# Attention transposes as 64-row halves, the last query tile's scores in 64-row form, and one written order for attention

## The chip, the cores and the metric

The kernel runs on one core of a Trainium2 chip. The metric is the device time of one execution in microseconds (us); the median of three runs of the kernel before is 1041.93 us (1041.54 to 1042.49).

## What is computed

Causal attention with a forget bias over 4 x 8 heads of 576 rows and 64 columns, then two feed-forward layers over the 2304 tokens.

```
B, H, S, D = q.shape                      # 4, 8, 576, 64
scores = scale * np.matmul(q, k.transpose(0, 1, 3, 2))
cum = np.cumsum(np.maximum(s, 0.0), axis=-1)
bias = -(cum[:, :, :, None] - cum[:, :, None, :])
scores = np.where(causal, -1000000000.0, scores + np.minimum(bias, 0.0))
attn = np.exp(scores - np.max(scores, axis=-1, keepdims=True))
attn = attn / (np.sum(attn, axis=-1, keepdims=True) + 1e-09)
attn_out = np.matmul(attn, v)
...
x = np.ascontiguousarray(attn_out.transpose(0, 2, 1, 3)).reshape(B * S, H * D)
x = (1.0 / (1.0 + np.exp(-(x @ w_gate))) * (x @ w_val)) @ w_out
h = x @ w_in
return (h * np.cos(h)) @ w_out2
```

## The kernel before

The program has two stages. `attention` handles 16 pairs of heads, two heads side by side on the 128 partitions. `moe` then runs both feed-forward layers; the change does not touch it.

For one pair p, the 576 query rows are cut into tiles t = 0 to 3 of 128 rows and t = 4 of 64 rows for each head, the two tails of the pair together. The operations have names, which the change's table uses:

- G loads q, k and v; PQ and PK transpose q (five 128 x 128 transposes, L554) and k (six of 96 rows, L551) on TensorE; H and L split the result into a high and a low part (QH, QL, KH, KL, 64 rows to a head). DB spreads the cumulated s over the partitions (CB).
- Z, ZA and ZM make bias and causal mask on GpSimd. A computes scores: A0 is t = 0 and 1, A2 and A3 are t = 2 and 3 (L629: 64 rows of each head, the two heads as two matmuls side by side). A4 is the last tile (L634: one matmul over all 128 rows, with q of the two heads in a block form).
- X adds the bias and takes the row's extreme on VectorE (L646); E is the exponential on ScalarE (L650), which also sums the row; T transposes the result (L688 and L690: 25 transposes to a pair, each one matmul of 128 identity columns over 128 rows). C copies a transposed tile from PSUM to `pt`, on ScalarE (L460) or VectorE (L464).
- V0 and V1 multiply with v (L725, L727: 128 rows, 64 output partitions to a head). U copies that out; RA, RC, RT, RR, RD, RB make the reciprocal of the sums, turn it (L740), write it to memory and read it back spread over the partitions; M divides; XH and XL split the result for `moe`.
- Early pieces of the first weights (w0, w1, w2) are decoded along with it, and 40 "fill" matmuls of 256 columns (L788) stand wherever the planner finds TensorE free; 2 "warm" groups and one group at L475 stand at the start.

What sets the order: `Plan.run` is a list scheduler. It takes, of all operations that could begin within 0.1 us of the earliest, the one of lowest priority number (PRIO, EARLY, the pair's number), and picks ScalarE, VectorE or GpSimd for it by planned end plus a toll. Every engine then executes its own operations in that order, waiting on semaphores. PSUM is eight banks, given out by `Banks` under limits by kind (LIMIT); a T takes one bank of its own, except that of t = 4, which takes two.

Of the kernel before, what the change touches and what calls it, by code (L numbers as in the profile page):

```python
# [24 lines left out]
INF = float("inf")  # L25
# [11 lines left out]
class Buf:  # L37


    def __init__(self, pool, n=1, kind=None):  # L40
        self.pool, self.n, self.kind, self.left, self.slots, self.end = pool, n, kind, 0, None, 0.0
        pool.order.append(self)
# [6 lines left out]
class Pool:  # L49
    def __init__(self, n, fifo=True):  # L50
        self.n, self.fifo = n, fifo
        self.free = [0.0] * n
        self.order, self.next = [], 0

    def when(self, buf):
        if self.fifo and self.order[self.next] is not buf:
            return INF, None
        ok = sorted((t, i) for i, t in enumerate(self.free) if t < INF)
        if len(ok) < buf.n:
            return INF, None  # L60
        return ok[buf.n - 1][0], [i for _, i in ok[:buf.n]]

    def take(self, buf):
        _, slots = self.when(buf)
        buf.slots = sorted(slots)
        for i in slots:
            self.free[i] = INF
        self.next += 1
# [6 lines left out]
class Banks(Pool):  # L75


    def __init__(self, n, limit):
        super().__init__(n, fifo=False)
        self.limit, self.held, self.kinds = limit, {}, {}  # L80

    def when(self, buf):
        free, held = self.free, self.held.setdefault(buf.kind, [])
        lim = self.limit[buf.kind]
        now = sum(1 for t in held if t == INF)
        if now >= lim:
            return INF, None
        at = sorted((t for t in held), reverse=True)[lim - 1] if len(held) >= lim else 0.0
        best = (INF, 0, [])
        for i in range(0, self.n, 2):  # L90
            a, b = free[i], free[i + 1]
            if buf.n == 2:
                best = min(best, (max(a, b, at), 0, [i, i + 1]))
            else:
                for x, y, z in ((a, b, i), (b, a, i + 1)):
                    best = min(best, (max(x, at), -y if y < INF else -1e9, [z]))
        return best[0], best[2]

    def take(self, buf):
        super().take(buf)  # L100
        held = self.held[buf.kind]
        buf.place = len(held)
        held.append(INF)

    def give(self, buf):
        super().give(buf)
        self.held[buf.kind][buf.place] = buf.end


class Op:  # L110
    __slots__ = ("name", "alts", "fn", "prio", "deps", "left", "ready", "begins", "bufs", "out", "unit", "start", "end", "n", "xfer")
# [3 lines left out]
LAT = {"pe": 0.24, "act": 0.16, "dve": 0.13, "pool": 0.08}  # L115


class Plan:
# [3 lines left out]
    def op(self, name, alts, fn, rd=(), wr=(), needs=(), prio=0.0, xfer=0.0):  # L122
        o = Op()
        o.name, o.alts, o.fn, o.prio, o.xfer = name, alts, fn, prio, xfer
        o.n, o.unit, o.start, o.end, o.ready = len(self.ops), None, None, None, 0.0
        deps = set()
# [12 lines left out]
        o.deps, o.left, o.out = deps, len(deps), []  # L139
        for d in deps:  # L140
            d.out.append(o)
        o.bufs = {k[0] if isinstance(k, tuple) else k for k in (*rd, *wr, *needs)}
        o.bufs = [b for b in o.bufs if isinstance(b, Buf)]
        o.begins = []
        for b in o.bufs:
            b.left += 1
            o.begins.append(b)
# [3 lines left out]
    def run(self, slack=0.1):  # L151
        free = {}
        dma = 0.0
        ready = [o for o in self.ops if o.left == 0]
        done = []
        while ready:
            best = None
            cand = []
            for o in ready:
                at = o.ready  # L160
                for b in o.begins:
                    if b.slots is None:
                        t, _ = b.pool.when(b)
                        at = max(at, t)
                if at == INF:
                    continue
                for u, dur in o.alts.items():
                    s = max(at, free.get(u, 0.0))
                    cand.append((s, o, u, dur))
            if not cand:  # L170
                raise RuntimeError("stuck: " + ", ".join(o.name for o in ready[:20]))

            by_op = {}
            for s, o, u, dur in cand:
                c = (s + dur + TOLL.get(u, 0.0), s, o, u, dur)
                if o.n not in by_op or c[0] < by_op[o.n][0]:
                    by_op[o.n] = c
            first = min(c[1] for c in by_op.values())
            _, s, o, u, dur = min((c for c in by_op.values() if c[1] <= first + slack), key=lambda c: (c[2].prio, c[1], c[2].n))
            for b in o.begins:  # L180
                if b.slots is None:
                    b.pool.take(b)
            o.unit, o.start = u, s
            free[u] = s + dur
            if o.xfer:
                dma = max(dma, s + dur) + o.xfer
                o.end = dma + 2.3
            else:
                o.end = s + dur
# [5 lines left out]
            ready.remove(o)  # L195
            done.append(o)
            for d in o.out:
                d.left -= 1
                same = not o.xfer and set(d.alts) == {u}
                d.ready = max(d.ready, o.end + (SAME.get(u, 0.05) if same else LAT.get(u, 0.1)))  # L200
                if d.left == 0:
                    ready.append(d)
        if len(done) < len(self.ops):
            raise RuntimeError("operations left")
        self.done = sorted(done, key=lambda o: (o.start, o.n))
        return self.done


TOLL = {"act": 0.7, "dve": 0.52, "pool": 0.05}
REPORT = None  # L210
W0PRIO = 4

PV_GROUPS = [(0, 1), (2, 3, 4)]

ORDER = [0, 2, 4, 3]
LIMIT = {"prep": 3, "s4": 6, "s": 3, "t4": 2, "t": 4, "v": 4, "r": 6}

PRIO = {
# [4 lines left out]
}  # L223

EARLY = [
    {
# [4 lines left out]
    },  # L231
    {
# [4 lines left out]
    },  # L237
]
WARM = 2
W0AT = 2  # L240
FILL = 40
# [3 lines left out]
def kernel(  # L245
# [168 lines left out]
    def attention():  # L414
        with ExitStack() as c2:
# [6 lines left out]
            OPS = {n: [att.tile([P, S + TAIL if n[0] == "Q" else S], F32R, name=f"{n}{i}") for i in range(NCC)] for n in ("QH", "QL", "KH", "KL")}  # L422
            CB = [[att.tile([P, 6 * P], F32, name=f"CB{e}{i}") for i in range(NCC)] for e in range(2)]
            VN = [att.tile([P, NQ, 2, D], F32, name=f"VN{i}") for i in range(NV)]
            QKN = {x: [att.tile([P, NQ, 2, D] if x == "Q" else [PP, 6, 2, D], F32, name=f"{x}n{i}") for i in range(NQK)] for x in "QK"}
# [18 lines left out]
            pl["pw"] = Banks(8, LIMIT)  # L444
            DMA = {"sp": 0.62}

            here = [2]

            def add(name, alts, fn, prio, rd=(), wr=(), needs=(), xfer=0.0):
# [3 lines left out]
                kind = re.match('[A-Za-z]*', name)[0]  # L453
                o = plan.op(name, alts, None, rd, wr, needs, prio + PRIO.get(kind, 0.0) + (EARLY[here[0]].get(kind, 0.0) if here[0] < 2 else 0.0), xfer)
# [11 lines left out]
            def half(e):  # L466
                return slice(64 * e, 64 * e + 64)

# [23 lines left out]
            def setup_tail(u):  # L492
                for i in range(NQK):
                    for e in range(2):
                        u.memset(QKN["Q"][i][half(1 - e), NT4, e], 0.0)
                for i in range(NV):
                    u.memset(VN[i][TAIL:P, NT4], 0.0)
                for i in range(NPT):
# [562 lines left out]
```

## Time and profile before

| | |
|---|---|
| median of the runs | 1041.93 us |
| the profiled execution | 1041.43 us, of which its span is 1039.6 us |
| attention: first matmul to first matmul of `moe` | 1.18 to 185.03 us |
| `moe` | 185.03 us to the end |
| busy over the span | TensorE 99%, VectorE 70%, ScalarE 45%, GpSimd 40% |
| granted TensorE clock, mean | 1.000 |

The ends of matmuls are modelled, so that a busy TensorE is not one at its peak: what a matmul costs is read from the start of one to the start of the next. A row of the timeline merges instructions of a line that follow each other, so the start of the next row minus its own start, divided by its count, is the cost of one.

### The profile page before, as it was taken

How to read it: one execution, taken by the hardware profiler on the slowest of the kernel's cores; microseconds unless marked ns; L12 is line 12 of the kernel's file. 1: busy time of each engine (PE TensorE's matmuls, PEld its weight loads, DVE VectorE, ACT ScalarE, POOL GpSimd, SP SyncE). 2: the span in 40 equal slices, each digit the busy share in tenths (PEclk: the TensorE clock that was granted, in tenths of full speed). 3: DMA queues.
4: the chain of work that ended last, by engine and by line, in shares of the span. 5: the costliest groups of instructions: out<-in, count | busy, mean ns of one | idle time of the engine just before them, and what ended most of it. 6: DMA issues, size and time to landing. Idle time of an engine off the chain costs nothing.

```text
span 1039.6 us, 16693 instructions
## 1 busy us (share of the span) xinstructions
PE 1029.1 (99%) x6116; PEld 945.9 (91%) x6116; DVE 730.8 (70%) x1406; ACT 472.2 (45%) x1060; POOL 413.2 (40%) x494
## 2 busy tenths in 40 slices
PE   9999999999999999999999999999999999999998
PEld 6776777999999999999999999999999999999997
DVE  7788898565645557744344887888688878886565
ACT  4878877342222222221121335666555455554443
POOL 3567776241222223321111234555255535552222
PEclk9999999999999999999999999999999999999999
DMA  7777784321111111111010111121021101100111
GB/s 170 174 194 166 185 188 103 93 81 41 42 41 41 61 41 61 62 46 37 21 41 21 42 61 61 41 61 61 1 61 41 61 21 42 61 1 13 49 61 61
DMA packets 94802, 70.49 MB, mean 68 GB/s; under 512 B 61888, under 2 KB 82752, under 8 KB 94720
## 3 DMA queue, kind: packets, MB, share of 16 engines
q1 hardware_dynamic: 93456, 69.06, 24.0%
q8 instruction: 48, 0.79, 0.3%
q10 hardware_dynamic: 1264, 0.37, 0.2%
q14 instruction: 34, 0.28, 0.1%
HBM read 64.54 MB, written 4.87 MB: 67 GB/s over the span
## 4 chain that ended last, share of the span: by engine, by line
PE 93%; DVE 2%; issue 2%; DMA 1%; POOL 1%; ACT 1%; SPq 0%; POOLq 0%; DVEq 0%; ACTq 0%
PE pw L381 21%; PE pw L380 21%; PE pw L382 20%; PE pw L908 6%; PE pw L909 6%; PE pw L910 6%; PE pw L727 3%; PE pw L688 3%; PE pw L629 3%; PE pw L634 1%; DMA rb<-rec_d 1%; PE pw L554 1%; PE pw L551 1%; DMA raw<-in_moe_w_gate_dram 0%; DVE pu L646 0%
## 5 line engine op out<-in xcount | busy, mean ns | idle before, releaser
L382 PE MATMUL pw<-XH,wp 128*128 128x384 f32 x960 | 322.7, 336 | 0.0
L381 PE MATMUL pw<-XL,wp 128*128 128x384 f32 x960 | 322.7, 336 | 0.0
L380 PE MATMUL pw<-XH,wp 128*128 128x384 f32 x960 | 322.5, 336 | 0.0
L335 POOL TENSOR_TENSOR wp<-wm,wp 128x512 fp32r<-128x512 f32 x68 | 101.5, 1493 | 228.7 <-DVE wp L334 226.0
L380 PEld LDWEIGHTS pw<-XH,wp 128*128 128x128 f32 x960 | 180.1, 188 | 3.7
L381 PEld LDWEIGHTS pw<-XL,wp 128*128 128x128 f32 x960 | 180.0, 188 | 3.6
L382 PEld LDWEIGHTS pw<-XH,wp 128*128 128x128 f32 x960 | 180.1, 188 | 0.0
L898 POOL TENSOR_TENSOR gl<-tm,gh 128x384 fp32r<-128x384 f32 x96 | 108.8, 1133 | 142.7 <-ACT gh L897 142.6
L327 POOL TENSOR_TENSOR wm<-wm,wx 128x512 int32<-128x512 int32 x68 | 90.4, 1329 | 181.6 <-DVE wm L326 181.6
L826 DVE TENSOR_TENSOR tm<-pw,tm 128x384 f32<-128x384 f32 x72 | 40.1, 557 | 148.8 <-PE pw L382 139.1
L908 PE MATMUL pw<-wp,gh 128*128 128x512 f32 x288 | 112.2, 389 | 0.0
L909 PE MATMUL pw<-wp,gh 128*128 128x512 f32 x288 | 112.1, 389 | 0.0
L910 PE MATMUL pw<-wp,gl 128*128 128x512 f32 x288 | 112.0, 389 | 0.0
L828 ACT CAST gh<-tm 128x384 fp32r<-128x384 f32 x72 | 37.0, 514 | 143.9 <-DVE tm L826 143.9
L883 DVE SCALAR_TENSOR_TENSOR tm<-tm 128x384 f32<-128x384 int32 x96 | 99.0, 1031 | 3.3
L884 ACT ACTIVATE tm<-tm 128x384 f32<-128x384 f32 x96 | 50.6, 527 | 108.9 <-DVE tm L883 108.9
L380 PE MATMUL pw<-gh,wp 128*128 128x384 f32 x288 | 96.7, 336 | 0.6 <-ACT acc L854 0.6
L381 PE MATMUL pw<-gl,wp 128*128 128x384 f32 x288 | 97.0, 337 | 0.0
L382 PE MATMUL pw<-gh,wp 128*128 128x384 f32 x288 | 96.2, 334 | 0.0
L314 ACT ACTIVATE wx<-wx,ebias 128x512 int32<-128x512 int32 x68 | 49.2, 723 | 99.9 <-DVE wx L313 98.8
L650 ACT ACTIVATE pu<-pu,nm 128x128 f32<-128x128 f32 (+3 forms) x144 | 82.8, 577 | 19.8 <-DVE nm L646 19.5
L891 DVE SCALAR_TENSOR_TENSOR tm<-tm,pw 128x384 f32<-128x384 f32 x96 | 52.8, 550 | 42.4 <-ACT tm L885 42.4
(102 smaller groups left out, 1721.0 us busy)
## 6 DMA issues: line engine op xcount, KB each, us to landing
raw<-in_moe_w_out_dram SPq DMA_DIRECT2D x28, 512.0 KB
CB<-cum_d SPq DMA_DIRECT2D x32, 288.0 KB
raw<-in_moe_w_in_dram SPq DMA_DIRECT2D x16, 512.0 KB
raw<-in_moe_w_gate_dram SPq DMA_DIRECT2D x12, 512.0 KB
raw<-in_moe_w_val_dram SPq DMA_DIRECT2D x12, 512.0 KB
VN<-in_v_dram SPq DMA_DIRECT2D x31, 160.0 KB
Kn<-in_k_dram SPq DMA_DIRECT2D x32, 144.0 KB
rb<-rec_d SPq DMA_DIRECT2D x32, 144.0 KB
```

What stands on the lines that cost most here:

```text
L327: pool.tensor_tensor(m, m, st["x"], ALU.add)
L335: pool.tensor_tensor(w[:, 1], m, f(w[:, 0]), ALU.subtract)
L380: pe.matmul(ps, wh, xh, start=first, stop=False)
L381: pe.matmul(ps, wh, xl, start=False, stop=False)
L382: pe.matmul(ps, wl, xh, start=False, stop=last)
L650: act.activation(o, o, AF.Exp, bias=NMT[nm.slot][:, col:col + 1], scale=-1.0, accum_out=SUMS[sums.slot][:, col:col + 1])
L883: dve.scalar_tensor_tensor(r, kk, -TWO_PI_LO, r, ALU.mult, ALU.add)
L891: dve.scalar_tensor_tensor(g, r, -0.5, h, ALU.add, ALU.mult)
L898: pool.tensor_tensor(gl, g, f(gh), ALU.subtract)
L908: pe.matmul(ps, gh[:, ts], w[:, 0], start=it["first"], stop=False)
L909: pe.matmul(ps, gh[:, ts], w[:, 1], start=False, stop=False)
L910: pe.matmul(ps, gl[:, ts], w[:, 0], start=False, stop=it["last"])
```

## The change

Four things change in `attention`, none in `moe`.

1. A transpose (`flip`) becomes two matmuls, one for rows 0 to 63 and one for rows 64 to 127, each with 64 identity columns and the same 128 stationary columns, into two neighbouring PSUM banks. It holds for T, RT and for q and k; k is loaded as 128 x 4 rows and a tail, and so has five transposes in place of six. Before, 400 T, 80 PQ, 96 PK and 16 RT are issued; after, 832 halves for T and RT and 320 for q and k.
2. The last tile's scores (A4) are twelve matmuls of 64 rows, six side by side, in place of six of 128 rows; they come in two halves, A4 and A5, and A5 stands behind T of t = 0 and 1 of the same pair, so that t = 4 is the last of the pair's tiles.
3. The scheduler, its priorities, the limits by kind and the 40 fillers go. A table SEQ names all operations of attention in one order, with the engine where there is a choice (`:a` ScalarE, `:d` VectorE, `:p` GpSimd). T of one group, both heads, shares one pair of PSUM banks.
4. Copies C read the two halves in one instruction; t = 1 takes two copies (one to a head) in place of one, t = 4 one of 640 columns in place of two. K's high and low parts are 640 columns wide in place of 576. K's load is three DMAs to a pair in place of two.

```
+            def flip(out, i, x):
+                for h in range(2):
+                    pe.transpose(out[:, h, i:i + 64], x[half(h)], ident[half(h), half(h)])
...
-                                u.dma_start(out=t, in_=src.rearrange("(c p) d -> p c d", p=PP))
...
+                            u.dma_start(out=t[:, 0:NT4, e], in_=src[e, 0:NT4 * P].rearrange("(p c) d -> p c d", c=NT4))
...
+                        if x == "K":
+                            u.dma_start(out=t[half(0), NT4], in_=src[:, NT4 * P:S].rearrange("e p d -> p e d"))
...
-                    def scores4(u, sc=sc, cc=cc):
-                        for z in range(2):
-                            for i, (a, b) in enumerate(SCP):
-                                pe.matmul(PW[:, sc[0].slot + z, 0:HS], OPS[a][cc.slot][:, NT4 * P:NT4 * P + P], OPS[b][cc.slot][:, z * HS:(z + 1) * HS], start=i == 0, stop=i == 2)
...
+                    def scores4(u, turn, sc=sc, cc=cc):
+                        for i, (a, b) in enumerate(SCP):
+                            for e in range(2):
+                                z = e ^ turn
+                                pe.matmul(PW[:, sc[0].slot + z, 0:HS], OPS[a][cc.slot][half(e), QCOL[NT4]:QCOL[NT4] + P], OPS[b][cc.slot][half(e), z * HS:(z + 1) * HS], start=i == 0 and turn == 0, stop=i == 2 and turn == 1)
...
+                        add(f"A5.{p}", "pe:400", parts[1], rd=[*ready, ("t01", p, 0), ("t01", p, 1)], wr=[sc4])
...
-                                        pe.transpose(o[:, c * P:(c + 1) * P], x[:, c * P:(c + 1) * P], ident)
...
+                                    for c in range(t + 1):
+                                        i = (TAIL + c * P) % S if t == NT4 else c * P
+                                        flip(o, e * (t + 1) * 64 + c * 64, x[:, i:i + P])
...
-            for i in range(FILL):
-                fill = Buf(pl["pw"], 1, "t")
...
-            done = plan.run()
...
+            for o in plan.run(SEQ):
                 o.fn()
```

Of the table, one line of 40:

```
+C0.3.0:d T0.4.0 E1.1.1 T0.2.0 Z1.2 T1.2.0 X1.3.1 E0.0.1 X0.3.1 E1.0.1 ZT1.2 C1.2.0:a C0.2.0:d T0.1.1 T0.0.1 A5.1 RA0 C0.1.1:d ZM1.2.1 ZM0.2.1 C0.4.0:a A2.1 C0.0.1:d V0.0
```

TensorE within the third pair. Names are output<-moving,stationary; `pu` is the exponentials, QH to KL the parts of q and k. Before:

```order
L634 MATMUL pw<-KL_86,QH_80 128x288
L688 MATMUL pw<-ident,pu_104 128x128 x3
L629 MATMUL pw<-KH_84,QH_80 128x512 x2
L629 MATMUL pw<-KH_84,QL_82 128x512 x2
L629 MATMUL pw<-KL_86,QH_80 128x512 x2
L688 MATMUL pw<-ident,pu_105 128x128 x3
L629 MATMUL pw<-KH_84,QH_80 128x384 x2
L629 MATMUL pw<-KH_84,QL_82 128x384 x2
L629 MATMUL pw<-KL_86,QH_80 128x384 x2
L554 MATMUL pw<-ident,Qn_93 128x128 x5
```

And after, between the scores A3 and A0 of one pair:

```order
L604 MATMUL pw<-KL_85,QH_79 128x512 x2
L444 MATMUL pw<-ident,pu_106 128x64 x8
L444 MATMUL pw<-ident,pu_103 128x64 x6
L610 MATMUL pw<-KH_83,QH_79 128x288 x2
L610 MATMUL pw<-KH_83,QL_81 128x288 x2
L610 MATMUL pw<-KL_85,QH_79 128x288 x2
L444 MATMUL pw<-ident,pu_107 128x64 x8
L444 MATMUL pw<-ident,pu_104 128x64 x6
L604 MATMUL pw<-KH_83,QH_79 128x128 x2
```

Before, each row of L634, L688 or L554 is over 128 rows of the array and each of L629 over 64; after, all rows of the piece are over 64. Counted over attention in the program's order, TensorE goes from 128-row to 64-row form or back 67 times before (three of them around fillers) and 3 times after (around warm groups), and to or from the 64-column form of V 37 times before and 39 after.

TensorE at the start. Before, the last fillers and what follows them:

```order
L788 LDWEIGHTS ident
L788 MATMUL pw<-ident 128x256
L629 MATMUL pw<-KH_84,QH_80 128x128 x2
L629 MATMUL pw<-KH_84,QL_82 128x128 x2
L629 MATMUL pw<-KL_86,QH_80 128x128 x2
```

And after, from the last warm matmul to the first transposes of exponentials:

```order
L487 LDWEIGHTS pu_110
L487 MATMUL pw<-pu_110 128x512
L604 MATMUL pw<-KH_83,QH_79 128x384 x2
L604 MATMUL pw<-KH_83,QL_81 128x384 x2
L604 MATMUL pw<-KL_85,QH_79 128x384 x2
L610 MATMUL pw<-KH_84,QH_80 128x288 x2
L610 MATMUL pw<-KH_84,QL_82 128x288 x2
L610 MATMUL pw<-KL_86,QH_80 128x288 x2
L444 MATMUL pw<-ident,pu_101 128x64 x8
```

Where 26 fillers stood between the scores of the first two pairs, there is one warm group and then scores; no matmul is there to fill a wait.

ScalarE, the copies of one pair's transposed tiles. Before:

```order
L460 COPY pt_98<-pw 128x2x2x128
L460 COPY pt_98<-pw 128x3x128 x2
L460 COPY pt_98<-pw 128x4x2x64
L460 COPY pt_98<-pw 64x2x64
L460 COPY pt_98<-pw 128x4x128 x2
```

And after:

```order
L433 COPY pt_97<-pw 128x2x128 x3
L433 COPY rr<-pw 9x128
L433 COPY pt_97<-pw 128x4x128
L645 ACTIVATE pu_103,sums_116<-pu_103,nm_119 128x384
L645 ACTIVATE pu_109,sums_116<-pu_109,nm_119 128x576
L433 COPY pt_97<-pw 128x3x128 x2
L433 COPY pt_97<-pw 128x2x5x64
```

The copies of t = 0 and 1 are three of 256 columns, that of t = 4 is one of 640. Counted over attention, ScalarE's copies to `pt` go from 36 of 512 columns, 19 of 384, 6 of 256 and 10 small ones to 24 of 512, 19 of 384, 35 of 256 and 13 of 640; VectorE's from 28, 13, 10 and 6 small ones to 8, 13, 13 and 3 of 640.

## Rows read from the trace of the kernel before

**Rows 1.** The chain that ended last, from the page: shares of the span by line
```profile
PE pw L381 21%; PE pw L380 21%; PE pw L382 20%; PE pw L908 6%; PE pw L909 6%; PE pw L910 6%; PE pw L727 3%; PE pw L688 3%; PE pw L629 3%; PE pw L634 1%; DMA rb<-rec_d 1%; PE pw L554 1%; PE pw L551 1%; DMA raw<-in_moe_w_gate_dram 0%; DVE pu L646 0%
```

**Rows 2.** Busy us by stretch: length, PE, PEld, DVE, ACT, POOL, granted clock, DMA
```profile
17.86:185.03 167.17, 163.32 (x1408) 120.87 (x1406) 143.90 (x419) 130.87 (x384) 112.82 (x236) 1.00 0.69 163
185.03:1039.60 854.57, 850.15 (x4612) 815.08 (x4608) 575.42 (x958) 335.58 (x662) 292.83 (x227) 1.00 0.15 47
```

**Rows 3.** Timeline of PE, one pair, 41.5 to 45.6: start us, us, instruction
```profile
41.52 0.60 PE L688 MATMUL pw<-ident,pu 128*128 128x128 f32 x4
42.05 0.33 PE L629 MATMUL pw<-KH,QH 64*128 64x128 f32 x2
42.22 0.28 PE L629 MATMUL pw<-KH,QL 64*128 64x128 f32 x2
42.33 0.28 PE L629 MATMUL pw<-KL,QH 64*128 64x128 f32 x2
42.44 0.33 PE L629 MATMUL pw<-KH,QH 64*128 64x256 f32 x2
...
42.93 0.40 PE L634 MATMUL pw<-KH,QH 128*128 128x288 f32 x1
43.17 0.29 PE L634 MATMUL pw<-KH,QL 128*128 128x288 f32 x1
43.30 0.29 PE L634 MATMUL pw<-KL,QH 128*128 128x288 f32 x1
...
43.83 0.49 PE L688 MATMUL pw<-ident,pu 128*128 128x128 f32 x3
44.25 0.49 PE L629 MATMUL pw<-KH,QH 64*128 64x512 f32 x2
44.58 0.39 PE L629 MATMUL pw<-KH,QL 64*128 64x512 f32 x2
44.81 0.40 PE L629 MATMUL pw<-KL,QH 64*128 64x512 f32 x2
45.14 0.55 PE L688 MATMUL pw<-ident,pu 128*128 128x128 f32 x3
45.62 0.44 PE L629 MATMUL pw<-KH,QH 64*128 64x384 f32 x2
```

**Rows 4.** Timeline of PE around a wait, 93.8 to 97.0
```profile
93.83 0.66 PE L551 MATMUL pw<-ident,Kn 96*128 96x96 f32 x6
94.32 0.82 PE L688 MATMUL pw<-ident,pu 128*128 128x128 f32 x6
96.40 0.28 PE L740 MATMUL pw<-ident,rc 128*9 128x128 f32 x1 [1.26 <-DVE rc L737]
96.52 0.62 PE L688 MATMUL pw<-ident,pu 128*128 128x128 f32 x4
96.97 0.27 PE L690 MATMUL pw<-ident,pu 128*64 128x128 f32 x1
```

**Rows 5.** Timeline of SP: K's two loads of a pair
```profile
14.95 1.02 SPq L535 DMA_DIRECT2D Kn<-in_k_dram  x2
```

**Rows 6.** Timeline of PE at the start: fillers, and the first transpose of exponentials
```profile
13.13 3.01 PE L788 MATMUL pw<-ident 128*128 128x256 bf16 x26
...
17.86 0.27 PE L688 MATMUL pw<-ident,pu 128*128 128x128 f32 x1
```

**Rows 7.** Groups by form, ACT, 17.86 to 185.03: busy us, mean ns, idle before
```profile
L460 ACT COPY pt<-pw 128x512 f32<-128x512 f32 x36 | 20.8, 586 | 8.1 <-PE pw L688 6.5 <-ACT pt L460 1.1
...
L460 ACT ACTIVATE QH<-pw 128x640 fp32r<-128x640 f32 x7 | 4.9, 702 | 1.0 <-PE pw L554 0.8
...
L460 ACT COPY pt<-pw 128x256 f32<-128x256 f32 x6 | 2.2, 365 | 1.5 <-PE pw L688 1.5
```

**Rows 8.** Groups by form, DVE, same stretch
```profile
L464 DVE COPY pt<-pw 128x512 f32<-128x512 f32 x28 | 19.2, 687 | 1.5 <-PE pw L688 0.7
...
L563 DVE SCALAR_TENSOR_TENSOR QL<-pw,QH 128x640 fp32r<-128x640 f32 x14 | 11.5, 821 | 1.2 <-ACT QH L460 1.1
```

**Rows 9.** Timeline of PE: the warm groups, before the clock rises
```profile
3.71 2.77 PE L511 MATMUL pw<-pu 128*128 128x512 bf16 x6
```

More of the change, by code (lines that the diff above doesn't have):

```diff
@@ L37, with __init__ @@
 class Buf:
[L40 to L42 removed]
+    def __init__(self, pool, n=1):
+        self.pool, self.n, self.left, self.slots, self.end = pool, n, 0, None, 0.0
     @property
@@ L49, with __init__, pick @@
 class Pool:
[L50 to L61, printed above, removed]
+    def __init__(self, n):
+        self.n, self.free = n, [0.0] * n
+    def pick(self, buf):
+        t, i = min((t, i) for i, t in enumerate(self.free))
+        return t, [i]
     def take(self, buf):
-        _, slots = self.when(buf)
-        buf.slots = sorted(slots)
-        for i in slots:
+        t, buf.slots = self.pick(buf)
+        if t == INF:
+            raise RuntimeError("no slot is free")
+        for i in buf.slots:
             self.free[i] = INF
-        self.next += 1
+        return t
     def give(self, buf):
@@ L75, with pick @@
 class Banks(Pool):
[L78 to L88, printed above, removed]
+    def pick(self, buf):
         best = (INF, 0, [])
         for i in range(0, self.n, 2):
-            a, b = free[i], free[i + 1]
+            a, b = self.free[i], self.free[i + 1]
             if buf.n == 2:
-                best = min(best, (max(a, b, at), 0, [i, i + 1]))
+                best = min(best, (max(a, b), 0, [i, i + 1]))
             else:
                 for x, y, z in ((a, b, i), (b, a, i + 1)):
-                    best = min(best, (max(x, at), -y if y < INF else -1e9, [z]))
+                    best = min(best, (x, -y if y < INF else -1e9, [z]))
         return best[0], best[2]
[L99 to L107, printed above, removed]
 class Op:
-    __slots__ = ("name", "alts", "fn", "prio", "deps", "left", "ready", "begins", "bufs", "out", "unit", "start", "end", "n", "xfer")
+    __slots__ = ("name", "alts", "fn", "deps", "ready", "bufs", "out", "unit", "start", "end", "n", "xfer", "mode")
 SAME = {"pe": 0.0}
 LAT = {"pe": 0.24, "act": 0.16, "dve": 0.13, "pool": 0.08}
+MODE = {"V": 1, "warm": 2}
+SWITCH = 0.15
 class Plan:
@@ L148, in op @@
         self.ops.append(o)
         return o
[L151 to L180, printed above, removed]
@@ new lines, in run @@
+    def run(self, seq):
+        names = {o.name: o for o in self.ops}
+        free, mode, dma, done = {}, 0, 0.0, []
+        for word in seq.split():
+            name, _, u = word.partition(":")
+            o = names.pop(name)
+            u = {"a": "act", "d": "dve", "p": "pool", "": next(iter(o.alts))}[u]
+            if any(d.end is None for d in o.deps):
+                raise RuntimeError(f"{name} comes too early")
+            s = max(o.ready, free.get(u, 0.0) + (SWITCH if u == "pe" and o.mode != mode else 0.0))
+            for b in o.bufs:
@@ new lines, in attention, with bias4_tail, bias4 @@
+                for e in range(2):
+                    pu = groups[NT4][3][NT4, e]
+                    def bias4_tail(u, e=e, cb=cb, pu=pu):
+                        later(u, PU[NT4][pu.slot][half(e), 0:TAIL], CB[e][cb.slot][half(e), NT4 * P:S])
+                    def bias4(u, e=e, cb=cb, pu=pu):
+                        u.tensor_copy(PU[NT4][pu.slot][half(e), TAIL:S], CB[e][cb.slot][half(e), 0:NT4 * P])
+                    add(f"ZT{e}.{p}", "pool:180", bias4_tail, rd=[(cb, e, 0)], wr=[(pu, e, "t"), ("z4", p, e)])
+                    add(f"ZA{e}.{p}", "pool:590", first[e], rd=[(cb, e, 0), ("z4", p, e)], wr=[(cb, e, 2)])
+                    add(f"Z{e}.{p}", "pool:650", bias4, rd=[(cb, e, 0)], wr=[(pu, e, "c"), ("z5", p, e)])
```

289 lines of the change are left out of this document (153 added, 136 removed), and 12 rows, old and new, of tables (EARLY, PRIO).

## The prediction

> **What bounds the kernel now.** I read the chain that ended last first [rows 1]: it is TensorE almost throughout, 80% of the span in the six lines of `moe` and some 12% in the lines of attention. `moe` is untouched and runs from 185.03 us to the end with TensorE busy 850 of 855 us [rows 2], so the change can act only by moving that start. In the stretch of attention from the first transpose of exponentials (17.86) to it, 167.17 us, TensorE is busy 163.32, VectorE 143.90 (86%), ScalarE 130.87 (78%) and GpSimd 112.82 (67%) [rows 2]. TensorE is the bound; VectorE is some 20 us behind it.
>
> A busy TensorE hides something, and the timeline of one pair shows it [rows 3]: what a matmul costs depends on whether the one before it used the array in the same form. In like company a 128-row transpose takes 0.11 us (four from 96.52 to 96.97 [rows 4]), and a pair of 64-row score matmuls takes 0.23 us for 512 columns (44.58 to 44.81) and 0.11 for 128 (42.22 to 42.33). At a change of form it takes more, before and behind. Into 64-row form: the three transposes at 43.83 last 0.42 in place of 0.33 (+0.09), and the first scores behind them 0.33 in place of 0.23 (+0.10), together 0.19. At 41.52 it is 0.53 for four, +0.09, and the first scores of 128 columns 0.17 for 0.11, +0.06, together 0.15. Into 128-row form: the scores at 44.81 last 0.33 for 0.23 (+0.10); the three transposes at 45.14 take 0.48, of which 0.33 is their own, 0.09 the next change and 0.06 the start, together 0.16. Where the last tile's scores come first the start is 0.24 for 0.13 (42.93 to 43.17 to 43.30), together about 0.20. So a change of form costs 0.15 to 0.20 us, and none of it shows as idle time.
>
> **The change, part by part.**
>
> *Changes of form removed.* By the program's order 67 changes between 128-row and 64-row form become 3, and 37 to or from the form of V become 39. At 0.17 the 64 are 10.9 us; the two more are 0.3 at the same price. **Minus 10.6 us**, on TensorE and therefore on the path; with the ends of the price 9.3 to 12.5.
>
> *The halved transposes.* Each pair of heads has 25 T, 10 for q and k and one RT: 36, over 16 pairs 576. No half of 64 rows and 64 columns is in the trace. Bound below: columns cost 0.082 us for 96 (six from 93.83 to 94.32 [rows 4]) and 0.11 for 128, thus some 0.055 for 64, if both halves run side by side and loading their weights costs nothing more. Bound above: two halves one after the other, each at the price of a whole one, 0.22. The nearest row is the scores of 128 columns [rows 3]: there too a step is two loads of 64 rows by 128 stationary columns and two short matmuls in two banks, and it takes 0.11 from 42.22 to 42.33, although 512 columns take only 0.23. The loads set that step, and they are the same here, so I take **0.11**: nothing gained or lost for T, q and RT. For k, five at 0.11 stand against six at 0.082: +0.05 to a pair, **plus 0.8 us**. The ends would be 576 x 0.055 = 32 us less or 576 x 0.11 = 63 us more.
>
> The Trainium skill, "TensorE: Matmul & The Clock Gate", section "LDWEIGHTS (loading the stationary operand)", gives a load as columns divided by 1.2 in ns, which is 107 ns for 128 columns whatever the rows. By it two loads in turn would make a half-and-half transpose 0.21 us, and the sum would be 60 us worse. The trace does not bear it out: two such loads and their matmuls fit into 0.11 us in the scores, and one load with its transpose of k into 0.082.
>
> *The last tile's scores.* Six of 0.13 [rows 3], 0.80, become six side-by-side pairs of 288 columns, which by the pairs of 128 and 512 columns lie near 0.14: nothing, within 0.1 us a pair. The halves A4 and A5 bring no change of form. A5, though, stands behind T of t = 0 and 1 in TensorE's queue, and these wait for exponentials; queued behind are the next pair's scores. That is part of the waits below.
>
> *The copies.* By the counts of the order and mean durations, ScalarE's copies to `pt` take 36 x 0.586 + 19 x 0.48 + 6 x 0.365 = 32.4 us and ten small ones of under 0.37, some 35 in all; after, 24 x 0.586 + 19 x 0.48 + 35 x 0.365 + 13 x 0.70 = 45 us (0.70 for 640 columns by the QH row, 0.48 for 384 between the rows of 256 and 512) [rows 7]: plus 10. VectorE loses 20 copies of 512 columns, 13.7 us [rows 8]. It gets three copies of 640 columns (2.5), three of 256 (some 1.1), 16 passes over K wider by a ninth (16 x 0.09) and, by the order, three more casts of K and four more steps of M, XH and XL, each at most the 0.82 of a 640-column pass: net about minus 3. If the stretch shrinks to 157 us, ScalarE is busy 141 of it (90%) and VectorE 141 (90%): neither is the bound, so none of this is on the path by itself, but the cover is thin, 16 us.
>
> *Loads.* One more DMA to a pair on SP at 0.5 us of issue [rows 5], 8 us over attention, in a queue whose loads are placed a pair ahead; nothing.
>
> *Start and waits.* At the start 26 fillers take 3 us [rows 6] in which TensorE has nothing to do until masks and exponentials are there; that chain (cumulated s, its spread, masks, X, E) is not shortened. Bounds are 3 us either way; I take 0. From 17.86 on, TensorE waits 167.17 minus 163.32 = 3.9 us [rows 2] plus 14 more fillers at 0.11, 1.5 us: 5.4 in all, with single waits such as the 1.26 us for the reciprocal at 96.40 [rows 4]. A written order may have fewer or, with both other engines at 90%, more; minus 4 to plus 7, and I take 0.
>
> *Sum.* Minus 10.6 plus 0.8 is minus 9.8: 1041.43 becomes 1031.6 for an execution like the profiled one (its span of 1039.6 and 1.8 around it). The median of the runs is 0.5 above the profiled one, so **1032.0** for the median, with 1028.5 to 1035.5 from the ends of the price and of the start and moderate waits.
>
> **Rivals.**
>
> *The order makes TensorE wait instead.* The gain lies on TensorE; the waits are decided by three engines' order, by four pairs of PSUM banks (every T group now holds two) and by a table that cannot react when a DMA is late. For it: ScalarE goes from 78% to 90%. Against it: even before, with everything dense, waits were 5.4 us. If they grow by 3.5 to 10 us, the time is 1035.5 to 1042; at 9.8 us more the whole gain is gone.
>
> *Halved transposes cost more* (slower than before). If two halves cannot share the array while loading, a flip is two steps of the k row, 2 x 0.082 = 0.165, and 576 x 0.055 = 32 us come on top: 1064. At the upper bound of 0.22, two whole steps in turn, it is 63 us: 1095. The point from which it decides is 9.8 / 576 = 0.017 us: at 0.127 us a flip there is no gain. Against it stands the 0.11 of the scores. The section on LDWEIGHTS named above leads to the second of these times.
>
> *Halved transposes cost less.* Near 0.055 TensorE would no longer be the bound; ScalarE's 141 us in a stretch that cannot begin before 13 us and ends with the last copies and V put the end of attention near 165 to 170 us: 1018 to 1028.
>
> *The clock falls.* The warm groups before 6.5 us take 2.77 us for six matmuls of 512 columns [rows 9], 0.46 each, twice the 0.23 of a pair later: TensorE starts at 1.2 GHz, and in the whole stretch from 17.86 it has 2.4 GHz, granted 1.00 [rows 2]. Before, fillers keep it working from 13.13 to 16.07 [rows 6]; after, it waits there. If the clock fell for as long as it was low at the start, some 5 us, 2.5 us would be lost, less where TensorE waits anyway: 1032 to 1035. If it fell again and again, each microsecond at the low level loses half of itself, and 20 us of that cancel the gain.
>
> *It does not do what it says*: the changes of form could stay if a half were built as a 128-row matmul; the order shows 64 identity columns and half the rows everywhere, so I give that nothing.
>
> **How the numbers follow.** The forecast, 1028.5 to 1035.5, has 0.63. More waits, 1035.5 to 1042, has 0.17, of which 0.05 lies within 2.1 us of 1041.9 and none above it by more. Dearer halves have 0.08, all slower (0.06 for 1064, 0.02 for 1095). Cheaper halves, or waits that nearly vanish, 0.07. The clock 0.05, most of it still faster. Faster by over 0.2% is then 0.63 + 0.12 + 0.07 + 0.04 = 0.86, within 0.2% (2.1 us, about what a measurement of this kernel can tell from no change) 0.05, slower 0.09. The range 1027 to 1038.5 holds the forecast, two thirds of the longer waits, and a little of the rest: 0.8.
>
> **What the profile after would show.** First, `moe` starts near 175 us. Second, in the timeline of a pair a group of eight halves takes 0.44 us, and scores behind it step by 0.23 and 0.11 from the first one on. Third, excess steps remain only around V. Fourth, ScalarE is busy near 90% of the stretch from the first transpose to `moe`, and idle TensorE there is 2 to 9 us. The prediction is wrong if halves step by other than 0.11, if idle time of TensorE grows past 10 us, or if the granted clock has stretches under 1.

## The result, and the profile after

The changed kernel takes **1053.47 us** (median of 4 runs, 1051.18 to 1055.97) against 1042.04 us before: a ratio of 1.011, 95% interval 1.0087 to 1.0134. It is 11.4 us slower; the prediction was 1032.0, at most 1038.5.

First the windows, in the columns of [rows 2]: the stage of attention, now from 17.86 to 196.88, and what follows.

```profile
17.86:196.88 179.02, 149.64 (x2036) 108.17 (x2036) 143.64 (x409) 138.42 (x407) 106.36 (x234) 0.95 0.63 154
196.88:1051.50 854.62, 850.13 (x4612) 815.10 (x4608) 577.85 (x962) 336.26 (x663) 295.08 (x228) 1.00 0.15 47
```

`moe` is what it was (854.62 us for 854.57) and starts 11.85 us later. TensorE's busy time fell from 163.32 to 149.64, 13.7 us less, and its idle time in the stage rose from 3.85 to 29.38 (179.02 minus 149.64), 25.5 us more. Work was saved, and nearly twice as much came back as waiting. VectorE and ScalarE are at 80 and 77% of the stage: no engine is at its limit.

What a transposed block costs, from the timeline of PE (start us, us, instruction):

```profile
20.32 0.71 PE L444 MATMUL pw<-ident,pu 64*128 64x64 f32 x16
20.84 0.48 PE L604 MATMUL pw<-KH,QH 64*128 64x512 f32 x2
```

Sixteen halves, eight blocks, go from 20.32 to 20.84: 0.065 us a block, against 0.11 whole [rows 4] and the 0.11 forecast. The records of the trace have the two halves of a block start some 0.002 us apart: they run side by side.

Scores between two groups of transposes, from the timeline further on:

```profile
84.80 0.50 PE L444 MATMUL pw<-ident,pu 64*128 64x64 f32 x10
85.09 0.49 PE L604 MATMUL pw<-KH,QH 64*128 64x512 f32 x2
85.41 0.40 PE L604 MATMUL pw<-KH,QL 64*128 64x512 f32 x2
85.64 0.40 PE L604 MATMUL pw<-KL,QH 64*128 64x512 f32 x2
85.87 0.35 PE L444 MATMUL pw<-ident,pu 64*128 64x64 f32 x6
```

In front of transposes the scores now take 0.23 us like any others (85.64 to 85.87; 0.33 before [rows 3]). Behind transposes the first ones still take 0.32 (85.09 to 85.41), although both are in 64-row form.

Where TensorE and its loads then wait, from the waits between 15 and 198 us (waiting line, what released it: us in total, times, longest):

```profile
PEld pw L444 <- ACT pt L433: 9.6, 14, 1.8
POOL wm L303 <- DVE wm L302: 7.6, 2, 6.2
PEld pw L444 <- DVE pt L437: 5.0, 6, 2.1
ACT wx L290 <- DVE wx L289: 5.0, 3, 3.5
PE pw L444 <- DVE pt L437: 4.2, 5, 2.0
PE pw L444 <- ACT pt L433: 4.2, 7, 1.1
PE pw L532 <- DMA Kn<-in_k_dram: 2.7, 1, 2.7
```

(PE and PEld are one wait seen at the matmul and at its load, so they are not added.) Transposes (L444) wait for copies (L433 on ScalarE, L437 on VectorE); ScalarE and GpSimd wait at L290 and L303, two parts of decoding a weight piece; and one load of k is late. Experiments follow on each.

The granted clock was 0.95 in the stage: five times TensorE ran at 1.2 GHz for about 3.4 us (from 97.2, 110.8, 141.6, 158.6 and 185.9 us). Shortly before the first four it had stood still for 1.3 to 2 us at one go, before the last only for shorter times; the longest wait, 2.72 us from 81.75 us, was followed by no fall.

### The profile page after: what moved, and what is told of

It reads as the page before. It is cut to its first block, busy times and chain, and to the rows that moved or that the text cites. A ratio compares the mean times of both kernels' runs of the same rounds, so it can differ in the third digit from the quotient of the medians.

```text
span 1051.5 us, 17900 instructions
## 1 busy us (share of the span) xinstructions
PE 1012.4 (96%) x6731; PEld 930.9 (89%) x6732; DVE 730.4 (69%) x1391; ACT 480.2 (46%) x1082; POOL 407.0 (39%) x487
## 4 chain that ended last, share of the span: by engine, by line
PE 80%; ACT 1%; DVE 1%; issue 1%; DMA 1%; POOL 1%; SPq 0%; DVEq 0%; POOLq 0%; ACTq 0%
PE pw L357 20%; PE pw L356 20%; PE pw L358 20%; PE pw L888 6%; PE pw L889 6%; PE pw L890 6%; DMA rb<-rec_d 1%; ACT pu L645 1%; POOL w L747 0%; DMA raw<-in_moe_w_gate_dram 0%; PE pw L444 0%; PE pw L604 0%; ACT pt L433 0%; DVE wm L298 0%; DVE pu L641 0%
## 5 line engine op out<-in xcount | busy, mean ns | idle before, releaser
L303 POOL TENSOR_TENSOR wm<-wm,wx 128x512 int32<-128x512 int32 x68 | 90.4, 1329 | 187.2 <-DVE wm L302 187.2
L290 ACT ACTIVATE wx<-wx,ebias 128x512 int32<-128x512 int32 x68 | 49.2, 724 | 103.3 <-DVE wx L289 102.3
L645 ACT ACTIVATE pu<-pu,nm 128x256 f32<-128x256 f32 (+3 forms) x144 | 83.1, 582 | 14.8 <-DVE nm L641 14.2
```

The costliest lines, as they stand in the source:

```text
L303: pool.tensor_tensor(m, m, st["x"], ALU.add)
L645: act.activation(o, o, AF.Exp, bias=NMT[nm.slot][:, col:col + 1], scale=-1.0, accum_out=SUMS[sums.slot][:, col:col + 1])
```

## The experiments

The theories: **order**, that the table makes engines wait for each other, at the decode above all; **halves**, that the new form itself is dear (its time on TensorE, or its banks); **clock**, that the falls of the clock cost the time. Each ratio is to the kernel before on the same chip.

**1. Every half issued twice** (halves, clock).

```
-                for h in range(2):
+                for h in (0, 1, 0, 1):
```

> The changed kernel with every halved transpose of T and RT issued twice (the second writes the same again), so that TensorE works more in the same order; nothing is left out. Theory clock (the falls to 1.2 GHz, 24 us in the profile after, are what costs): the extra work keeps the clock up, granted clock near 1.00 after the start, and the time falls by 6 us or more, to 1047 or less. Theory order (the engines wait for each other in a fixed order, TensorE has slack): the clock may rise, but the time stays within 3 us of 1053.

Measured: 1057.97 us, ratio 1.0159 (1.0143 to 1.0174), some 5 us more than the changed kernel. Neither number was met: the clock theory wanted 1047 or less, the order theory was nearer with 3 us around 1053. The stage by the windows (columns of [rows 2], here and in the experiments below):

```profile
17.86:199.98 182.12, 163.27 (x2851) 126.32 (x2848) 143.31 (x405) 138.42 (x404) 105.89 (x231) 1.00 0.61 152
```

TensorE is as busy as before the change and at 1.00 in the whole stage, and the stage is 15 us longer than before: without one fall of the clock. Only about 3 of the 13.6 us of extra work show in the stage's length; what the clock gave back is in that difference too.

**2. Whole 128-row transposes in the same written order**, each head's block in a bank of its own, for t = 0 and 1 each tile's (halves).

```
...
-                                        flip(o, e * (t + 1) * 64 + c * 64, x[:, i:i + P])
+                                    pe.transpose(o[:, at + c * P:at + (c + 1) * P], x[:, i:i + P], ident)
...
```

> The changed kernel with T as whole 128-row transposes again, 0.11 us each, in the same written order and the same PSUM pairs; RT, q, k and the last tile's scores stay as halves. Theory clock: TensorE is busier and the clock stays up, 1045 or less although some 80 changes of form come back. Theory order: the time stays at 1050 or more. If the halved form itself cost something in the copies that read two banks, the copies to pt would be shorter here by a tenth.

Measured: 1049.09 us, ratio 1.0074 (1.0059 to 1.0089). The windows:

```profile
17.86:193.37 175.51, 165.87 (x1637) 117.73 (x1637) 142.92 (x407) 138.01 (x405) 106.69 (x232) 0.99 0.63 157
```

TensorE works 16 us more and the stage is 3.5 us shorter, so something that is not TensorE's work costs time with the halves. The time lies between the two theories' ranges, and the interval of its ratio overlaps slightly with that of the changed kernel. ScalarE's copies of 512 columns are as long as with halves (0.584 us for 0.586), so it is not their length. The clock fell once in place of five times and may be a part of it; experiment 7 tests the banks apart from it.

**3. The decode of the weight pieces at the end of the order** (order): the 18 words `w0fetch` to `w2split` behind all others.

> The changed kernel with the 18 steps that fetch and decode the three weight pieces moved from the middle of the written order to its end, so that moe must wait for them; all else in the same order. Theory decode (their ScalarE and GpSimd parts, which the order has no place for, block those queues from 80 us on): the last V of attention ends at 188 us or before, against 196.9, though the whole gets no faster since moe starts only when the pieces are there. Theory clock or theory order alone: the last V ends within 3 us of 196.9.

Measured: 1056.66 us, ratio 1.0146. The windows of attention and of the gap behind it:

```profile
17.86:184.54 166.68, 144.43 (x2029) 104.16 (x2025) 132.60 (x391) 134.74 (x402) 97.02 (x226) 0.98 0.65 156
184.54:194.60 10.06, 0.00 (x1) 0.00 (x0) 5.60 (x10) 2.03 (x3) 2.65 (x2) 0.65 0.31 98
```

Attention ends 12 us earlier (184.54 for 196.9), and then TensorE stands still for 10 us, since `moe` needs the pieces. That is the theory of the decode. In the middle of the order the decode costs attention 12 us, its own work and the waits behind it together.

**4. The kernel before without its 40 fillers** (`FILL = 0`; the clock).

> The kernel before without its 40 fillers. Theory clock: the granted clock falls at the start, after 13 us, where the fillers stood, and the time rises by 1 to 4 us. If the fillers do nothing, the clock stays at 1.00 and the time stays within 1 us of 1042.

Measured: 1038.42 us, ratio 0.997 (0.9959 to 0.9982), with a granted clock of 1.00 in the stage: about 3 us faster, which neither theory had. The clock did not need the fillers. But the planner, without them, also lays the other operations in another order, so the 3 us are not the price of the fillers alone.

**5. The hidden parts of the decode in places of their own** (order). In the table a word like `w1exponent` is one VectorE operation, but it also issues a ScalarE instruction; `sign` and `split` issue GpSimd ones. What that does at 141 to 146 us of the changed kernel, on ACT and on DVE:

```profile
141.03 0.19 ACT L645 ACTIVATION_READ_ACCUMULATOR pu<-pu,nm 128x1 f32 x1
144.72 0.72 ACT L290 ACTIVATE wx<-wx,ebias 128x512 int32<-128x512 int32 x1 [3.50 <-DVE wx L289]
145.35 0.90 ACT L433 COPY pt<-pw 128x256 f32<-128x256 f32 x3
```

```profile
142.56 0.82 DVE L437 CAST KH<-pw 128x640 fp32r<-128x640 f32 x1
143.42 0.82 DVE L543 TENSOR_TENSOR KL<-pw,KH 128x640 fp32r<-128x640 f32 x1
144.16 0.47 DVE L289 TENSOR_SCALAR wx<-raw 128x512 int32<-128x512 int32 x1
```

ScalarE reaches L290 at 141.2 and stands 3.5 us at the head of its queue for a result that VectorE delivers at 144.63, behind KH and KL; three copies that attention wants wait behind it. TensorE then waits 0.81 us for those copies.

Of the three kinds one is shown here; each gets a word of its own in the table:

```
-            act.activation(x, x, AF.Relu, bias=ebias[e], scale=8.0)
...
+        def rebias():
+            act.activation(st["x"], st["x"], AF.Relu, bias=ebias[e], scale=8.0)
```

> Same operations, same written order, but the parts of a weight piece that run on ScalarE and GpSimd (one and two per piece, nine in all), which in the changed kernel are issued together with the VectorE part before them, get words of their own and stand up to 16 words later, where the VectorE part is nearly done. Theory 'blocked queues': in the changed kernel ScalarE waited 5.0 us in three places and GpSimd 7.6 us in two at the head of their queues for these parts, and the work behind them (copies and exponentials, masks) came late; then the attention stage gets 4 to 8 us shorter and the time is 1045 to 1050 us. Theory 'VectorE load': it is the 10 us of VectorE work in the pieces that delays, wherever the other parts stand; then 1052 to 1055 us, no change.

Measured: 1045.99 us, ratio 1.0044 (1.0027 to 1.006). Nine instructions moved by 0 to 16 words give 7 us back (0.0066 of 1041, with some 3 us of uncertainty), and in the trace the waits at the head of the two queues, 5.0 us on ScalarE and 7.6 on GpSimd in the changed kernel, are gone. Blocked queues are shown, and by the medians are some 60% of the slowdown. Two of the five falls of the clock went with them, at most 3.4 us of the 7 if each microsecond at 1.2 GHz loses half (an estimate).

**6. All operations of the change in another written order** (order against halves): the words of SEQ permuted, 94 of the 224 operations that have a choice of engine given to the other one, and else only the edit of experiment 5.

> The operations of the changed kernel, each with the same instructions (halved transposes, 64-row scores, halved preps, same copies), in another written order: the words of the table are permuted, some copies go to the other engine, and the parts of a weight piece have words of their own. Nothing is added or taken out. Theory 'the written order': TensorE's idle time of 29.4 us in the attention stage comes from the order alone, and with another order most of it goes; the last V product ends before 187 us (196.9 in the changed kernel, 185.1 before) and the time is 1034 to 1043 us. Theory 'the operations': the halved forms bring the waits with them (two banks held by each transpose, copies that gather from two banks), whatever the order; then 1048 us or more.

Measured: 1039.49 us, ratio 0.9987 (0.9977 to 0.9996). The windows:

```profile
17.86:181.43 163.57, 145.50 (x2025) 106.21 (x2021) 136.00 (x408) 137.53 (x396) 110.02 (x234) 0.97 0.69 168
```

The same operations take 15.5 us less of attention, and the loss turns into a small gain. The last V product ends at 181.5 us, as the theory of the order had it. The order, with its choice of engines, is the cause of the slowdown; the operations are not. It also had three falls of the clock (from about 17, 51 and 96 us), so these do not decide the sign.

**7. Why the halves ask for another order: two heads in the same banks.** The copies of the two heads' tiles t = 3 of pair 4, from four timelines: ACT and DVE of the changed kernel, then ACT and DVE of experiment 2:

```profile
61.57 0.57 ACT L433 COPY pt<-pw 128x512 f32<-128x512 f32 x1
```

```profile
62.17 0.69 DVE L437 COPY pt<-pw 128x512 f32<-128x512 f32 x1 [0.43 <-ACT pt L433]
```

```profile
62.97 0.57 ACT L433 COPY pt<-pw 128x512 f32<-128x512 f32 x1
```

```profile
62.67 0.69 DVE L437 COPY pt<-pw 128x512 f32<-128x512 f32 x1
```

With halves VectorE's copy starts 0.03 us after ScalarE's has ended; with each head in its own bank the two overlap. They share no data: one reads head 0's block and the other head 1's, but halves put both blocks into the same two banks. The wait is in the program: VectorE's copy waits for a semaphore that ScalarE's copy releases. Over the stage, from the waits of the changed kernel:

```profile
ACT pt L433 <- DVE pt L437: 2.4, 5, 1.0
DVE pt L437 <- ACT pt L433: 2.2, 5, 0.6
```

In the waits of experiment 2 there is no such line.

The Trainium skill, "PSUM — Partial Sum Buffer", section "PSUM bank collisions raise a hardware error", says that no two of TensorE, VectorE and ScalarE may work in one bank on the same partitions at once, two reads included, and that software has to keep them apart. The trace agrees: the two copies above are serialised, 0.03 us apart.

The test keeps experiment 2's whole transposes, order and copies, and only spreads both heads' blocks over the same two banks, in two of the three shared groups:

```
-                                at = 512 * (t if t < 2 else e)
+                                    at = {0: 512 * c, 1: 512 * (c % 2) + P + P * (c // 2), 2: 512 * e + c * P, 3: 512 * (c // 2) + P * (2 * e + c % 2), 4: c * P}[t]
...
```

> The first experiment with whole transposes (a2_whole: first written order, one whole transpose for a block, each head's blocks in a bank of its own, 1049.1 us) with one thing changed: in two of the three groups that two heads share (the query tiles 3, and 0 with 1) the blocks of both heads are spread over the same two banks, as the halves spread them; transposes, copies, their sizes and their order stay. Theory 'shared banks': a copy by one engine has to wait while the other engine copies out of the same bank, and a transpose while a copy reads its bank; then ScalarE's copies wait for VectorE's and the other way round, as in the changed kernel, and the time is 3 to 8 us longer than with whole transposes in separate banks, 1052 to 1057 us. Theory 'no matter': what made the halves slower there was something else in them, and the time stays within 1 us of 1049.

Measured: 1054.59 us, ratio 1.0126 (1.0113 to 1.0139), 5.4 us more than experiment 2 (0.0052 of 1041). The windows:

```profile
17.86:198.53 180.67, 166.62 (x1636) 116.28 (x1634) 142.26 (x407) 137.95 (x405) 107.20 (x232) 1.00 0.63 152
```

Its copies wait for each other again:

```profile
DVE pt L437 <- ACT pt L433: 2.5, 4, 1.0
ACT pt L433 <- DVE pt L437: 1.2, 3, 0.5
```

The copies' lengths did not change (0.585 us for 0.584 at 512 columns on ScalarE). So the shared banks alone cost the 5.4 us in this order. The clock was 1.00 in the stage, and the kernel is as slow as the changed one, with 17 us more work on TensorE.

**8. A third order, and whole transposes in it**: SEQ permuted once more, now without the two warm groups at the start; then the edit of experiment 2 in that order.

> The operations of the changed kernel once more, in a third written order, put together from the durations that the traces of these runs show (a 64-row half transpose at 0.03 us, a copy at its measured length), and without the two groups of three fillers at the start (the run of the kernel before without its fillers kept a granted clock of 1.00). Theory 'the written order': the last V product ends at 171 to 176 us (181.5 in the second order, 185.1 before) and the time is 1028 to 1035 us, faster than both kernels. Theory 'something else binds': the stage can't get under the 163.6 us it took in the second order, because VectorE and ScalarE (136 and 138 us busy of it) are at their limit; then 1037 to 1041 us. If the missing fillers let the clock fall in the stage, that shows as a granted clock under 0.97 between 18 us and the last V product.

> The third written order, with each transposed block as one whole 128-row transpose into one bank (the two heads' blocks in separate banks) in place of two 64-row halves side by side; all else as in the third order. In the first order this form was 4.4 us faster than the halves although it costs TensorE twice the time. Theory 'the halves are the cheaper form once TensorE is what the order waits for': 288 transposes of 9 chunks to a head, some 16 us more of TensorE time (165.9 against 149.6 us busy in the first order), lengthen the stage: 5 to 14 us slower than the halves in the same order. Theory 'banks': a half transpose has to wait until both banks of its pair are copied out, so whole ones are faster in any order, by 2 to 5 us.

Measured: 1043.36 us, ratio 1.0015 (1.0005 to 1.0025), and 1047.01 us, ratio 1.0042 (1.0027 to 1.0056). Both theories on the third order missed: it is neither faster than both kernels nor bound by VectorE or ScalarE (142.22 and 134.79 us busy of 167.24). The last V product ended at 183.6. In its trace ScalarE's copies wait 13.4 us in all for VectorE's, and VectorE's 3.8 us for ScalarE's, as in experiment 7; that is one cause of its loss. In one and the same order halves are 3.65 us faster than whole transposes, shared banks and all: the theory of the cheaper form holds in sign and is below its size. The order was laid out with the durations of halves, which may favour them.

**9. Orders that respect the banks, and the load queue**: two more permutations of SEQ, both without the warm groups, the second also with a buffer table made from measured durations; and the fourth order with K's third load left out from the third pair on, whose last 64 keys are then those of an earlier pair:

```
...
-                        if x == "K":
+                        if x == "K" and p < NQK:
                             u.dma_start(out=t[half(0), NT4], in_=src[:, NT4 * P:S].rearrange("e p d -> p e d"))
```

> The operations of the changed kernel (halves, shared banks, no change to any instruction but the two groups of three fillers at the start, left out) in a fourth written order. It is put together like the third, from measured durations, but with the further rule that two engines don't work on the same two banks at once: a copy waits for the other engine's copy from its banks, and a transpose for the copies from them. Theory 'order and shared banks': the third order came out 10 us longer than it was laid out for because that rule was missing; with it the last V product ends at 168 to 174 us (183.6 in the third order, 185.1 before) and the time is 1026 to 1033 us, faster than both kernels. Theory 'something else binds': the stage stays above 163 us in any order and the time is 1037 us or more.

> A fifth written order of the changed kernel's operations, without the fillers at the start, laid out with the shared-bank rule and with the load queue (SP) at its measured pace, 0.65 us from one load to the next (the fourth order left SP 15 us of its 152 in the stage, and GpSimd waited 18.3 us for loads of CB); the table that hands out the buffers uses the same measured durations. Theory 'order': with the loads placed in time the last V product ends at 174 to 178 us (179.7 in the fourth order) and the time is 1031 to 1036 us. Theory 'all five queues are full by now': whatever the order, the stage stays near 162 to 164 us and the time is 1037 to 1040 us.

> The fourth written order with the third load of K (its last 64 rows, one DMA to a pair that the change added on SP) left out from the third pair on, so that the last 64 keys are those of an earlier pair; all else as in the fourth order. It frees 14 x 0.65 = 9 us of the load queue. Theory 'the load queue holds the stage': loads of CB come earlier, GpSimd waits less than 18 us for them, and the time falls by 2 to 6 us, to 1032 to 1036 us. Theory 'the extra load costs nothing', as the prediction had it: 1038 us, within 1 us.

Measured: the fourth order 1038.28 us, ratio 0.9964 (0.9949 to 0.9978); the fifth **1035.51 us, ratio 0.9948 (0.9936 to 0.9961)**, faster than both kernels; the fourth without k's third load 1034.47 us, ratio 0.9943 (0.9927 to 0.996). The fifth leaves out fillers and warm groups too, and the kernel before without its fillers had 0.997 (experiment 4): what is left for the change itself is 0.0022, 2.3 us, and there the intervals touch. GpSimd's largest wait for loads, from the waits of the fourth order, of the same without that load, and of the fifth:

```profile
POOL pu L640 <- DMA CB<-cum_d: 18.3, 8, 9.7
```

```profile
POOL pu L640 <- DMA CB<-cum_d: 10.6, 3, 8.1
```

```profile
POOL pu L660 <- DMA CB<-cum_d: 8.2, 6, 2.5
```

In the fourth order the last V product ended at 179.7, 6 us past the range expected of it, and the time fell into the range of the rival theory; ScalarE's and VectorE's copies no longer wait for each other in its trace (17.2 us in the third), and GpSimd waited for loads of CB. From one load to the next SP takes some 0.65 us, and between 17.86 and 170 us it spent 130 of 152 us issuing them. Without k's extra load the waits for CB fall from 18.3 to 10.6 us (in all, with a second line for CB, from 23.2 to 17.6) and the time by some 2 us, but the two intervals overlap, so the size is not settled. The fifth order ends V at 178.9, and with 161 us its stage is under the 162 to 164 of the rival theory; its windows:

```profile
17.86:178.85 160.99, 144.21 (x2032) 105.82 (x2030) 143.52 (x411) 138.12 (x408) 97.98 (x225) 0.98 0.68 171
```

TensorE still idles 16.8 of 161 us, VectorE is busy 89% of it. Of 19 us less busy time on TensorE than before, the stage keeps 6.

## Why the prediction was wrong, step by step

- **What bounds the kernel.** Right for the kernel before, and right that only `moe`'s start can move. But "TensorE is the bound" was true of that kernel's order. Shorten its work, and waits for the other engines and for loads decide: TensorE idles 29.4 us in the changed kernel and 16.8 in the fifth order.
- **Changes of form, minus 10.6 us.** Right in part. In front of transposes the excess is gone (0.23 us for 0.33). Behind them the first scores still take 0.32 in place of 0.23, though the prediction had them at 0.23 "from the first one on": that excess stays without a change of rows, and why is not shown. The last block of a group is some 0.03 us shorter (ten halves in 0.29), which leaves about 0.06 at each of the 54 passages in the trace, some 3.5 us of the 10.6 (an estimate from these steps).
- **The halved transposes, 0.11 us.** Mis-sized: 0.065, next to the lower bound of 0.055 that I set aside; over 576 blocks that is 26 us. Two 64-row loads and their matmuls fit into it side by side. TensorE's busy time fell by less, 13.7 us; a row of two halves is modelled as 0.22 us long where the next block can follow after 0.065, so short waits count as busy. The Trainium skill, "TensorE: Matmul & The Clock Gate", section "LDWEIGHTS (loading the stationary operand)", would have a single such load take 0.107; the trace does not agree here either. The error lay on the harmless side: I forecast too little gain on TensorE and the time still rose.
- **Waits, 0 with minus 4 to plus 7. This is the step that failed.** Idle time in the stage grew by 25.5 us, which undid the gain and left 11.4 us on top. I named the ingredients in a rival (three engines' order, pairs of banks, a table that can't react) and gave them 3.5 to 10 us and 0.17, by extending the 5.4 us of a planned order to another order. Two things could have been read beforehand. The words for the decode hide ScalarE and GpSimd instructions, and an instruction at the head of a queue holds all behind it: 7 us (experiment 5). And halves put both heads into the same banks, which by the program's waits keeps two copies, or a copy and a transpose, from running together: 5.4 us, measured with whole transposes (experiment 7). I counted the banks as space and not as something only one engine may use at a time.
- **Copies, off the path.** ScalarE's busy time rose by 7.6 us for the 10 forecast, VectorE's stayed (minus 3 forecast). Not their sum put them on the path, but the waits above: in the changed kernel transposes wait 8.4 us for copies.
- **Loads, nothing.** Not shown to be nothing. In the changed kernel TensorE waits 2.7 us for a k load at 84.5 us. These are its three DMAs:

```profile
77.64 1.28 SPq L508 DMA_DIRECT2D Kn<-in_k_dram  x2
80.15 0.63 SPq L512 DMA_DIRECT2D Kn<-in_k_dram  x1
```

  By its semaphores that wait ended with the second of the first two, which landed at 84.33; the added third landed at 84.53. So this wait is not the third load's, and what the third costs stays open (experiment 9).

- **The clock.** The rival happened in form: five falls of about 3.4 us in the stage, and 1.2 GHz from 8.4 to 15.3 us. The early one delays nothing that shows: the first transpose of exponentials starts at 17.56 us, and at 17.86 before. The falls alone are not why the kernel is slower: experiments 1 and 7 have 1.00 throughout the stage and are as slow, though with 14 and 17 us more work on TensorE, and experiment 6 has three falls and is faster. How much the five cost was not measured; if each microsecond at 1.2 GHz loses half (a pair of scores of 512 columns takes 0.43 us there, 0.23 at 2.4 GHz), it is at most 8.5 us, less than the 11.4.
- **Cheaper halves: 1018 to 1028.** The condition came nearly true (0.065 for 0.055), the time did not, in any of five orders.

What stays open: of the 16.9 us between the changed kernel and the fifth order (0.0162 of 1041), the decode's places and the banks were measured at 7 and 5.4 in different settings, and the rest (late loads, clock, warm groups, other waits) was not separated.

## What to carry to other kernels

When a change takes work from the engine that bounds a stage and also rewrites the order, forecast the idle time as carefully as the work: go through each queue for instructions that will wait at its head, and for each PSUM bank ask which engines will want it at the same moment. A layout that costs TensorE 0.065 us in place of 0.11 came out behind one that keeps two readers in different banks in the first order, and ahead of it in the third. And test the order apart from the operations: the same operations, two warm groups apart, ranged in five orders from 1035.5 to 1053.5 us.

## What the runs showed of the hardware

Two 64-row transposes side by side take 0.065 us for a whole 128 x 128 block in fp32, where one 128-row transpose took 0.11. The first scores behind a group of transposes take 0.09 us more than the next ones, with 64-row transposes (0.32 for 0.23) as with 128-row ones (0.33 for 0.23).

The granted clock fell to 1.2 GHz for some 3.4 us at a time in the changed kernel, four times of five shortly after a wait of 1.3 us or more. It stayed at 2.4 GHz in the whole stage of the kernel before without fillers, where TensorE hardly waits (161.08 us busy of 165.14, its windows):

```profile
17.86:183.00 165.14, 161.08 (x1381) 117.88 (x1379) 141.87 (x415) 132.05 (x388) 111.17 (x234) 1.00 0.68 164
```

One more small DMA to a pair lengthens a queue that issues one every 0.65 us: without it SP spent 120 us in place of 130 on issuing (17.86 to 170 us), and GpSimd waited 5.6 us less for loads of CB. What that is worth in time is not settled.
